# Seed stores and the second unit's queries on GpSimd's DMA queue, and earlier loads of the first unit's operands

## The chip, the cores and the metric

One Trainium2 chip; the kernel runs on 1 of its 8 cores. The metric is device time in microseconds, lower is better.

## The reference

Two independent blocks, whose results are laid side by side. Block A is an S4D convolution: kernels K are built from complex exponentials and convolved with u by FFT. Block B is attention with 16 heads of 28 dimensions over 2048 positions, without a mask. All data are float32.

```python
# A: L = 2048, D = 448, N = 256
dt = exp(log_dt);  A = -exp(log_A_real) + 1j * A_imag;  C = (C_real + 1j * C_imag) * dt[:, None]
P = exp((A * dt[:, None])[:, :, None] * arange(L))
K = 2 * einsum("dn,dnl->dl", C, P).real
y = irfft(rfft(u_t, 2 * L) * rfft(K, 2 * L))[:, :, :L]      # then y + u * D_skip
# B: S = 2048, D = 448, H = 16
q, k, v = split(x @ wqkv)
p = softmax(q @ k.T * 28 ** -0.5)
b = (p @ v) @ wo
out = concatenate([a, b], axis=-1)
```

## The kernel before

The work has an opening and a main loop.

**The main loop** goes over 16 units. A unit u is one group g of four heads (G = 4 groups) and one chunk c of 512 queries (NQ = 4 chunks), and each unit takes 16 steps over tiles of 128 keys. In a step, TensorE makes the scores of four heads (`s_mm`), ScalarE takes their exponentials, and TensorE multiplies the previous step's exponentials with v (`pv_step`). Alongside run the row maxima of the next unit (`max_mm`), the S4D kernels (`k_start`, `e_power` on GpSimd, `g_powers` on VectorE, `k_mm`), and the FFT stages of block A. Its instructions are kept in program order.

**The opening** has two streams. In it the order is not that of the program: a scheduler orders each engine's queue, SyncE's queue of DMA issues included.

- *Projections.* For each chunk of 512 positions (`c` in 0..3), `transposes` turns x, `qk_proj` makes keys and queries of the four groups as a high and a low part (`hl`, two buffers), and `v_proj` makes v. They are stored to DRAM (`k_d`, `q_d`, `v_d`); chunks 0 and 1 also give the key differences `kd_d` (tile `dhl`). Forty-eight such jobs are spread over the first `PW` = 37 of 41 slots.
- *Seeds.* In eight groups (`seeds(o)`, four slots apart) the first powers of the complex exponentials are made. GpSimd makes the sizes `tri` (mg), the first products (`e_base`, `g_base`) and the last complex products (`e5`, tiles `qhat` and `x_e`); ScalarE the sines and exponentials; VectorE the phases and the rest. A group's results lie in two tiles: `se`, a buffer of the pool of query tiles (name `qhat`, three buffers, shared with the queries proper), and `sg` (two buffers). `put_e` and `put_g` store them to `sd_d`, from where the main loop reloads them as `sdb`.

At the end of the opening the operands of the first unit are loaded: `load_kd` (key differences, tiles `kdif0` to `kdif3`), `load_q` (queries, tile `qhat`), `load_k` (keys, tile `khat`, four tiles of four loads each; two tiles from ScalarE's queue, two from SyncE's). `ahead[A0 + i]` and `ahead[A1 + i]` say in which slots the key differences and the first queries are issued. Then come the maxima of unit 0: 16 query tiles of 128 rows, four matmuls each (`max_mm`), of which three are reduced on VectorE. The negated maxima are written into two rows of the queries (`max_put`), and the main loop begins.

In the profile every recorded operation has line 75, that of a helper; operations are told apart by their tiles. SyncE's queue is "SPq", GpSimd is "POOL".

Of the kernel before, what the change touches and what calls it, by code (L numbers as in the profile page):

```python
# [8 lines left out]
F32 = mybir.dt.float32  # L9
F32R = mybir.dt.float32r  # L10
# [13 lines left out]
HG = H // G  # L24
CQ = 512
NQ = L // CQ
# [14 lines left out]
PS = 1  # L41
SGB, XB, XL = 2, 5, 4
K0, KP, KD, UP = 0, 3.5, 5, 3
A0, A1 = 26, 34

N1 = 32
N2 = 64
# [9 lines left out]
F_G = 256  # L57
# [33 lines left out]
def body(ctx, tc, a, out):  # L91
    nc = Engines(tc)
# [4 lines left out]
    def pool(stack, name, bufs=1, space=None, side=None):  # L97
        kw = {} if space is None else {"space": space}
        if side:
            kw["side"] = side  # L100
        return stack.enter_context(tc.tile_pool(name=name, bufs=bufs, reuse_waits="tile", **kw))
# [3 lines left out]
    kd_d = [dram.tile([2, 128, CQ], F32, name=f"kd_{g}") for g in range(G)]  # L105
    q_d = [[dram.tile([2, 128, CQ], F32, name=f"q_{g}_{c}") for c in range(NQ)] for g in range(G)]
    sd_d = [dram.tile([BO, 128, SDF], F32, name=f"sd_{o}") for o in range(NO)]
# [24 lines left out]
    kd_p = pool(att, "kd_p", side="right")  # L132
# [8 lines left out]
    kt_g, kd_g, q_u, m_u, mh_u, o_u, rl_u = {}, {}, {}, {}, {}, {}, {}  # L141

    def load_k(g, j, p, queue=nc.sync):
        t = p.tile([128, L], F32R, name="khat", bufs=HG)
        for r in range(4):
            queue.dma_start(t[32 * r:32 * r + 32, :].bitcast(F32), k_d[g][r % 2, 32 * j:32 * j + 32, :])
        kt_g.setdefault(g, []).append(t)
# [3 lines left out]
    def load_v(g, c):  # L151
        v_g[g, c] = t = v_p.tile([128, NK // NQ, HG, 32], F32, name="v", bufs=5)
        nc.sync.dma_start(t.rearrange("p t h e -> p t (h e)"), v_d[c][:, g])

    def load_kd(g, j, rows=range(4)):
        if 0 in rows:
            kd_g[g, j] = kd_p.tile([128, CQ], F32R, name=f"kdif{j}")
        t = kd_g[g, j]
        for r in rows:
            nc.sync.dma_start(t[32 * r:32 * r + 32].bitcast(F32), kd_d[g][r % 2, 32 * j:32 * j + 32, :])  # L160

    def load_q(u, rows=range(4)):
        g, c = divmod(u, NQ)
        if 0 in rows:
            q_u[u] = q_p.tile([128, HG, CQ], F32R, name="qhat", bufs=3)
        t = q_u[u]
        for r in rows:
            nc.sync.dma_start(t[32 * r:32 * r + 32].bitcast(F32), q_d[g][c][r // 2].rearrange("(j p) q -> p j q", j=HG))

    def max_mm(u, i, kc, ps=w_tile):  # L170

# [37 lines left out]
    with ExitStack() as st:  # L209
# [50 lines left out]
        t = a["A_log_dt"]  # L260
# [51 lines left out]
        def seeds(o):  # L312

            q = {}
# [92 lines left out]
            def cmul(e, dst, s0, n, wr, wi, conj):  # L407

                if e is nc.vector:
                    x_ = ps_x.tile([128, CQ], F32, name="px")[:, :BO * 16 * n].rearrange("p (b h e) -> p b h e", h=16, e=n)  # L410
                else:
                    x_ = s_p.tile([128, BO, 16, 4], F32, name="x_e")[:, :, :, :n]
                br, bi = (w_[:, :, :, None].to_broadcast([128, BO, 16, n]) for w_ in (wr, wi))
                for c in range(2):
                    mul(e, dst[c], s0[c], br)
                    mul(e, x_, s0[1 - c], bi)
                    e.tensor_tensor(dst[c], dst[c], x_, ALU.add if (c == 0) == conj else ALU.subtract)
# [2 lines left out]
            e8 = lambda *i: sl(q["e8"], *i)  # L420
            e3 = lambda: cmul(vec if o % 8 < E3 else pol, e8(3, 4), e8(1, 2), 1, q["e8"][:, :, 0, :, 2], q["e8"][:, :, 1, :, 2], False)
            e5 = lambda: cmul(pol, e8(5, 8), e8(1, 4), 3, q["e8"][:, :, 0, :, 4], q["e8"][:, :, 1, :, 4], False)
            put_e = lambda: nc.sync.dma_start(sd_d[o][:, :, :F_G].rearrange("b p f -> p b f"), q["se"])
            put_g = lambda: nc.sync.dma_start(sd_d[o][:, :, F_G:].rearrange("b p f -> p b f"), q["sg"])

            def load():
                if o not in nats:
# [68 lines left out]
        for c in range(NQ):  # L496
# [4 lines left out]
            if c + 1 < NQ:  # L501
                jobs[1] = (lambda c, f: lambda: (load_x(c + 1), f())[1])(c, jobs[1])
            work += jobs
        stages = [seeds(o) for o in range(NO)]
        n_stage = SP * (NO - 1) + len(stages[0])
        slots = [[] for _ in range(n_stage)]
# [4 lines left out]
        pend, n_work = [], len(work)  # L511

        ahead = collections.defaultdict(list)
        for i in range(2 * HG):
            ahead[A0 + i].append(lambda i=i: load_kd(0, i // 2, range(2 * (i % 2), 2 * (i % 2) + 2)))
        for i in range(2):
            ahead[A1 + i].append(lambda i=i: load_q(0, range(2 * i, 2 * i + 2)))

        def project():

            e = work.pop(0)() if work else None
            while pend:
                pend.pop(0)()
            if e:
                pend.append(e)

        for t in range(n_stage):
            while work and n_work - len(work) < n_work * (t + 1) / PW:
                project()
            for f in slots[t] + ahead.get(t, []):  # L530
                f()
            if t + 1 == PW:
                project()
                wst.close()
                k0_p = pool(k0_st, "k0_p", side="right")
                for j in range(HG):
                    load_k(0, j, k0_p, nc.scalar if j < 2 else nc.sync)
                load_q(1)
                for c in range(NQ):
                    load_v(0, c)  # L540
        xst.close()
        more = [lambda: ps_t.tile([128, CQ], F32, name="pt")] * 2 + [w_tile] * 3
        for i in range(16):
# [444 lines left out]
    for s in range(NS):  # L988
        u, kt = divmod(s, NK)
# [15 lines left out]
        if sm < NS and sm // NK % NQ == NQ - 1 and sm % NK % 4 == 0 and sm % NK and sm // (NQ * NK) + 1 < G:  # L1005
            load_kd(sm // (NQ * NK) + 1, sm % NK // 4 - 1)
        if sm < NS and sm % (NQ * NK) == 0 and sm:
            load_kd(sm // (NQ * NK), HG - 1)
        if kt % 4 == 1 and u % NQ == 1 and u // NQ + 1 < G:
            load_k(u // NQ + 1, kt // 4, k_pools[(u // NQ + 1) % 2])  # L1010
        if kt == 2:
            if u + 2 < NU:
                load_q(u + 2)
# [97 lines left out]
```

## Time and profile before

| | us |
|---|---|
| median of 3 runs | 1360.99 (1358.85 to 1361.72) |
| profiled execution | 1363.72 |
| its span in the trace | 1361.9 |

| engine | busy us, share of the span |
|---|---|
| PE (TensorE matmul) | 1243.9, 91% |
| DVE (VectorE) | 991.3, 73% |
| ACT (ScalarE) | 966.1, 71% |
| POOL (GpSimd) | 839.5, 62% |

Busy shares are means over stages with different limits, so the views that follow are taken by stretches of time. All DMAs of compute data are issued from SyncE's queue, but for eight key loads from ScalarE's. A row of a timeline gives start and duration in us, engine, operation, output tile and input tile, a count, and in brackets the idle time of that engine before it and what ended it. A row of a queue (SPq, ACTq) is the issue of a DMA, not its transfer.

### The profile page before, as it was taken

The page shows a single profiled execution, that of the slowest core. Times are in us where ns is not written, and L with a number is a line of the kernel's source. Part 1 is how long each engine was busy: PE and PEld are TensorE (multiplying, and loading weights), DVE is VectorE, ACT ScalarE, POOL GpSimd, SP SyncE. Part 2 cuts the span into 40 slices and gives each one's busy share as a digit, 9 for nine tenths or more (in the row PEclk, how much of TensorE's full clock was granted, in tenths as well). Part 3 has the DMA queues.
Part 4 walks back from the last instruction along what each step waited for, and adds up shares of the span by engine and source line. Part 5 has one row for each costly group of instructions (what it writes and reads, how often), then busy time and mean ns, then how long its engine had stood idle before and what let it go on. Part 6 is the DMA issues. An engine that isn't in the chain of part 4 may idle for free.

```text
span 1361.9 us, 33142 instructions
## 1 busy us (share of the span) xinstructions
PE 1243.9 (91%) x12625; PEld 709.8 (52%) x12625; DVE 991.3 (73%) x2138; ACT 966.1 (71%) x2067; POOL 839.5 (62%) x705
## 2 busy tenths in 40 slices
PE   6878885799999999999999999999998999998997
PEld 5657762455555555555555555555555545544433
DVE  5897886877777777777788888888887766857311
ACT  4876752488888888888888887878786655655553
POOL 3685681278877878878888988888895111202221
PEclk9988987899999999999999999999999999999999
DMA  6677669636675545378534233632325534636476
GB/s 197 199 261 266 225 212 271 179 74 150 147 164 118 128 135 159 111 202 198 162 94 97 56 73 86 146 79 67 79 65 140 189 116 161 206 111 203 138 192 176
DMA packets 200089, 205.36 MB, mean 151 GB/s; under 512 B 95993, under 2 KB 158521, under 8 KB 197881
## 3 DMA queue, kind: packets, MB, share of 16 engines
q1 hardware_dynamic: 199544, 201.13, 53.2%
q10 hardware_dynamic: 384, 2.10, 0.6%
q8 instruction: 100, 1.64, 0.5%
q14 instruction: 61, 0.49, 0.1%
HBM read 120.73 MB, written 82.18 MB: 149 GB/s over the span
## 4 chain that ended last, share of the span: by engine, by line
PE 61%; DVE 17%; ACT 12%; issue 3%; DMA 3%; POOL 3%; SPq 0%; ACTq 0%; DVEq 0%; POOLq 0%
PE pm L75 35%; PE po L75 13%; PE pss L75 12%; ACT p L75 6%; DVE mx L75 4%; DVE g L75 2%; DVE tri L75 2%; ACT rl L75 2%; DVE p L75 2%; POOL qhat L75 1%; DVE pr L75 1%; DVE zg L75 1%; DVE rl L75 1%; DVE sg L75 1%; ACT tri L75 1%
## 5 line engine op out<-in xcount | busy, mean ns | idle before, releaser
L75 ACT ACTIVATE p<-pss 128x512 f32<-128x512 f32 x1024 | 565.4, 609 | 138.5 <-PE pss L75 127.5
L75 PE MATMUL pss<-qhat,khat 128*128 128x512 f32 x1024 | 403.1, 400 | 3.3 <-ACT p L75 3.3
L75 DVE TENSOR_REDUCE mx<-pm 128x1 f32<-128x512 f32 x500 | 321.4, 683 | 116.3 <-PE pm L75 115.1
L75 PE MATMUL pm<-khat,qhat 128*128 128x512 f32 x749 | 330.1, 444 | 41.4 <-DVE mx L75 36.5
L75 POOL TENSOR_TENSOR e<-e,sdb 128x256 f32<-128x256 f32 x168 | 201.8, 1201 | 171.9 <-ACT e L75 162.9
L75 PE MATMUL po<-p,v 128*32 128x512 f32 x2048 | 271.9, 599 | 0.0
L75 POOL TENSOR_TENSOR e<-e,eu 128x256 f32<-128x256 f32 x168 | 248.1, 1477 | 13.2
L75 PEld LDWEIGHTS pm<-khat,qhat 128*128 128x128 f32 x749 | 142.0, 190 | 216.0 <-DVE mx L75 79.8
L75 PEld LDWEIGHTS pss<-qhat,khat 128*128 128x128 f32 x1024 | 191.1, 189 | 46.7 <-ACT p L75 11.2
L75 DVE CUSTOM_DVE_ANT_0 rl<-pm,rl 128x512 f32<-128x512 f32 x249 | 171.4, 688 | 48.3 <-ACT rl L75 43.8
L75 POOL TENSOR_TENSOR eu<-e,sdb 128x256 f32<-128x256 f32 x168 | 201.7, 1201 | 0.0
L75 DVE TENSOR_TENSOR g<-g,zg 128x128 f32<-128x128 f32 x392 | 162.9, 416 | 46.3 <-ACT zg L75 41.3
L75 ACT ACTIVATE rl<-pm 128x512 f32<-128x512 f32 x249 | 151.2, 607 | 20.7 <-PE pm L75 18.8
L75 POOL TENSOR_TENSOR p<-pr,pr 64x448 f32<-64x448 f32 x32 | 40.9, 1277 | 191.6 <-DVE pr L75 180.5
L75 PE MATMUL pm<-kdif,qhat 128*128 128x512 f32 x249 | 101.6, 408 | 2.2 <-DVE mx L75 1.5
L75 PEld LDWEIGHTS pm<-e,g 128*32 128x32 f32 x3584 | 63.0, 110 | 52.8 <-issue 30.8
L75 DVE TENSOR_TENSOR zg<-g,zg 128x128 f32<-128x128 f32 x224 | 87.5, 391 | 1.9
L75 PEld LDWEIGHTS po<-p,v 128*32 128x32 f32 x2048 | 56.6, 110 | 42.7 <-issue 38.0
L75 PE MATMUL pm<-xh,wh 112*128 112x512 f32 x128 | 56.8, 448 | 22.3 <-DVE hl L75 10.8
L75 PE MATMUL pm<-e,g 128*32 128x64 f32 x3584 | 72.5, 220 | 0.0
L75 ACT ACTIVATE y<-pm 128x448 f32<-128x448 f32 x48 | 26.3, 548 | 63.0 <-PE pm L75 30.7
L75 DVE TENSOR_TENSOR pr<-pm,ub 128x448 f32<-128x448 f32 x64 | 37.0, 619 | 32.7 <-PE pm L75 32.7
(137 smaller groups left out, 1571.8 us busy)
## 6 DMA issues: line engine op xcount, KB each, us to landing
sdb<-sd SPq DMA_DIRECT2D x56, 336.0 KB
qhat<-q SPq DMA_DIRECT2D x64, 256.0 KB
khat<-k SPq DMA_DIRECT2D x56, 256.0 KB
sd<-sg SPq DMA_DIRECT2D x8, 1456.0 KB
k<-hl SPq DMA_DIRECT2D x16, 512.0 KB
q<-hl SPq DMA_DIRECT2D x16, 512.0 KB
mw<-in_mw SPq DMA_DIRECT2D x16, 512.0 KB
sd<-qhat SPq DMA_DIRECT2D x8, 896.0 KB
```

Source lines behind the costliest of these rows:

```text
L75: i = f(*args, **kw)
```

## The change

- `put_e` and `put_g` issue the seed stores from GpSimd's queue instead of SyncE's (16 stores). So do the four loads of the second unit's queries, `load_q(1)`.
- The key differences of all four heads lie in one tile. Those of the first group are loaded by four loads, each for all heads, instead of sixteen; those of the later groups as before, head by head, into slices of that tile.
- The first key differences are issued from slot 27 on (before: from slot 26 in eight pieces), the first queries from slot 25 (before: 34).
- `load_q(1)` and the four `load_v(0, c)` stand behind the loop over the slots, ahead of the maxima, instead of inside it behind the key loads.

As the scheduler orders the opening's queues, the change moves more than its lines. In the new order the loads of v stand on SyncE's queue directly behind the stores of the chunk they read, the first one ahead of the second chunk's stores. All first-unit query loads stand ahead of the last chunk's key stores. On GpSimd the stores stand between the products, and the memsets of a group's seeds stand shortly behind the store whose buffer they reuse. In the main loop the order changes only at its first steps: the row maxima's store into the queries (`qhat<-mh`) stands behind two seed reloads, eight loads of u and one query row of unit 2.

```diff
-A0, A1 = 26, 34
+A0, A1 = 27, 25
...
-    def load_kd(g, j, rows=range(4)):
-        if 0 in rows:
-            kd_g[g, j] = kd_p.tile([128, CQ], F32R, name=f"kdif{j}")
-        t = kd_g[g, j]
-        for r in rows:
-            nc.sync.dma_start(t[32 * r:32 * r + 32].bitcast(F32), kd_d[g][r % 2, 32 * j:32 * j + 32, :])
-
-    def load_q(u, rows=range(4)):
+    kd_t = kd_p.tile([128, HG, CQ], F32R, name="kdif")
+
+    def load_kd(g, j):
+        kd_g[g, j] = kd_t[:, j, :]
+        for r in range(4):
+            nc.sync.dma_start(kd_t[32 * r:32 * r + 32, j, :].bitcast(F32), kd_d[g][r % 2, 32 * j:32 * j + 32, :])
+
+    def load_kd_row(r, g=0, t=kd_t):
+
+        kd_g.update({(g, j): t[:, j, :] for j in range(HG)})
+        nc.sync.dma_start(t[32 * r:32 * r + 32].bitcast(F32), kd_d[g][r % 2].rearrange("(j p) q -> p j q", j=HG))
+
+    def load_q(u, rows=range(4), queue=nc.sync):
...
-            nc.sync.dma_start(t[32 * r:32 * r + 32].bitcast(F32), q_d[g][c][r // 2].rearrange("(j p) q -> p j q", j=HG))
+            queue.dma_start(t[32 * r:32 * r + 32].bitcast(F32), q_d[g][c][r // 2].rearrange("(j p) q -> p j q", j=HG))
...
-            put_e = lambda: nc.sync.dma_start(sd_d[o][:, :, :F_G].rearrange("b p f -> p b f"), q["se"])
-            put_g = lambda: nc.sync.dma_start(sd_d[o][:, :, F_G:].rearrange("b p f -> p b f"), q["sg"])
+            put_e = lambda: nc.gpsimd.dma_start(sd_d[o][:, :, :F_G].rearrange("b p f -> p b f"), q["se"])
+            put_g = lambda: nc.gpsimd.dma_start(sd_d[o][:, :, F_G:].rearrange("b p f -> p b f"), q["sg"])
...
-        for i in range(2 * HG):
-            ahead[A0 + i].append(lambda i=i: load_kd(0, i // 2, range(2 * (i % 2), 2 * (i % 2) + 2)))
+        for i in range(4):
+            ahead[A0 + i].append(lambda i=i: load_kd_row(i))
         for i in range(2):
             ahead[A1 + i].append(lambda i=i: load_q(0, range(2 * i, 2 * i + 2)))
...
                 for j in range(HG):
                     load_k(0, j, k0_p, nc.scalar if j < 2 else nc.sync)
-                load_q(1)
-                for c in range(NQ):
-                    load_v(0, c)
+        load_q(1, queue=nc.gpsimd)
+        for c in range(NQ):
+            load_v(0, c)
         xst.close()
```

## The prediction

> **What bounds the kernel now.** I read the page first, then the windows of the opening stretch, then the queues in it.
>
> ```profile
> span 1361.9 us, 33142 instructions
> ...
> PE 61%; DVE 17%; ACT 12%; issue 3%; DMA 3%; POOL 3%; SPq 0%; ACTq 0%; DVEq 0%; POOLq 0%
> ...
> 60.75:198.00 137.25, 113.37 (x490) 90.69 (x489) 114.78 (x191) 95.03 (x194) 97.72 (x107) 0.90 0.71 239
> ...
> 200.00:210.00 10.00, 4.31 (x16) 3.10 (x15) 7.31 (x17) 1.28 (x2) 6.83 (x8) 0.84 1.02 332
> ...
> 209.00:218.00 9.00, 0.15 (x1) 0.18 (x2) 0.00 (x0) 0.95 (x4) 0.00 (x0) 0.50 1.04 243
> ...
> 218.00:252.00 34.00, 26.86 (x68) 13.23 (x68) 30.04 (x67) 9.78 (x17) 0.00 (x0) 0.89 0.93 259
> ```
>
> The columns of a window are its length, busy time of PE, weight loads, DVE, ACT and POOL, granted clock, DMA share, GB/s. Over the whole span the matrix engine carries the chain. The change touches only what comes before the main loop, about 258 us of 1361.9. That part has three pieces: projections and seeds to 208 us, where PE and DVE are each busy for over 80% of the time and no engine alone bounds; a hole from 209 to 218 where every engine stands and the DMA share is 1.04; then the 48 maxima of the first unit on DVE (30.04 of 34 us). The hole is where this change can earn something.
>
> ```profile
> 203.91 0.40 PE L75 MATMUL pm<-xl,wh 112*128 112x512 f32 x1
> ...
> 217.85 0.77 PE L75 MATMUL pt<-kdif,qhat 128*128 128x512 f32 x1 [13.54 <-DMA qhat<-q]
> ...
> 207.73 0.69 DVE L75 TENSOR_TENSOR hl<-pm,hl 128x512 fp32r<-128x512 f32 x1 [0.44 <-ACT hl L75]
> ...
> 219.50 1.29 DVE L75 TENSOR_REDUCE mx<-pm 128x1 f32<-128x512 f32 x2 [11.09 <-PE pm L75]
> ...
> 199.84 0.47 SPq L75 DMA_DIRECT2D qhat<-q  x1
> 200.74 0.49 SPq L75 DMA_DIRECT2D q<-hl  x1
> 201.28 0.51 SPq L75 DMA_DIRECT2D sd<-sg  x1
> 210.57 0.80 SPq L75 DMA_DIRECT2D qhat<-q  x2
> 211.46 0.38 SPq L75 DMA_DIRECT2D k<-hl  x1
> 211.94 0.42 SPq L75 DMA_DIRECT2D sd<-qhat  x1
> ...
> 215.45 2.60 SPq L75 DMA_DIRECT2D khat<-k  x2
> ...
> 204.11 1.60 ACTq L75 DMA_DIRECT2D khat<-k  x2
> ...
> 207.12 9.75 ACTq L75 DMA_DIRECT2D khat<-k  x5
> ```
>
> The last projection product ends at 204.3 and DVE is done with what precedes the maxima at 208.4. The first matmul of the maxima waits 13.54 us for the queries. Their last two rows stood on SP's queue behind the seventh group's seed store: SP issued it at 201.28 and could issue nothing until 210.57. The first key loads on ACT's queue, the other thing the maxima need, took from 204.11 until 216.87 to be issued.
>
> **Part by part: the tail.** The new order has all four query rows and all four key-difference rows of the first unit on SP's queue a chunk earlier, before the last keys are projected. No seed store remains on SP, so the key and query stores and the key loads follow each other directly. What is late next is the first key tile: four loads that ACT starts at 204.11.
>
> ```profile
> sd<-sg SPq DMA_DIRECT2D x8, 1456.0 KB
> ...
> sd<-qhat SPq DMA_DIRECT2D x8, 896.0 KB
> ...
> khat<-k ACTq DMA_DIRECT2D x8, 256.0 KB
> ...
> qhat<-q SPq DMA_DIRECT2D x64, 256.0 KB
> ```
>
> Those four loads are 1.05 MB. The two windows above move 332 and 243 GB/s; I take 289. The seventh group's seeds (896 and 1456 KB) still travel at that moment, from another queue. If the two queues share evenly, the loads take 2.1 MB / 289 GB/s = 7.3 us and are there at 211.4, 6.4 us before 217.85. If nothing shared, they would take 3.6 us and the end of DVE's earlier work, 208.4, would be the limit: 9.5 us. I take 6.4. Each further key tile has to come within a quarter of the 34 us window, 8.5 us; at the halved rate it needs 7.3, so the maxima keep their pace and the gain passes on to the main loop.
>
> ```profile
> 251.67 1.26 SPq L75 DMA_DIRECT2D qhat<-mh  x2
> ...
> L75 PE MATMUL pss<-qhat,khat x5: 398/449/632, 258.3 to 261.7; 128*128 128x512 f32 x5
> ```
>
> The maxima's rows are put into the queries at 251.67, and the first score product starts at 258.3. In the new order that store stands behind the seed reloads, the eight loads of u and one query row of the third unit, which waits for the last seed store. It is harmless as long as POOL's last store lands before about 245.
>
> **SP's waits before that.** Without seed stores, SP waits less for POOL and DVE, and stores of keys leave earlier.
>
> ```profile
> ACT hl L75 <- DMA k<-hl: 3.0, 1, 3.0
> ...
> 171.85 7.83 SPq L75 DMA_DIRECT2D v<-vst  x2
> ...
> 180.92 0.39 SPq L75 DMA_DIRECT2D k<-hl  x1
> ...
> 186.19 0.67 ACT L75 ACTIVATE hl<-pm,kones 128x512 fp32r<-128x512 f32 x1
> ...
> 60.75 4.12 DMA sd<-qhat
> ```
>
> In 60 to 209 us ACT waited 3.0 us for a key store to release a buffer. I credit half, 1.5 us, between nothing and all. Against it: the v loads no longer come behind the key loads; the scheduler puts them as soon as their stores are issued, and each one makes SP wait until the last v store has landed. For the last v chunk, the store issued at 179.7 is followed by such a load, with the key store of 180.92 behind it. With a landing time of 4.1 us, as the seed store's 4.12, that key store goes at 183.8 and lands at 187.9. Its buffer is wanted at 186.19, so 1.7 us at most; I take 1.4, since the v store is smaller. Below nothing it cannot go, as a wait is only added. The four joined key-difference loads replace sixteen small ones off the path: nothing.
>
> **POOL's queue.** This is the price. Sixteen stores and four query loads now stand between POOL's products, in order. Each of POOL's stalls is passed on: DVE waits for POOL's products, PE for DVE's evictions.
>
> ```profile
> L75 SPq DMA_DIRECT2D sd<-qhat x8: 360/513/1276, 60.7 to 237.7; - x8
> ...
> L75 POOL TENSOR_TENSOR qhat<-qhat x15: 1014/1161/3600, 55.3 to 203.7; 128x336 f32<-128x336 f32 x15
> ...
> 61.54 0.67 POOL L75 TENSOR_TENSOR gz<-tri 128x224 f32<-128x224 f32 x1 [0.82 <-DVE px L75]
> 62.17 1.46 POOL L75 TENSOR_TENSOR qhat<-tri 128x112 f32<-128x112 f32 x3
> ...
> 64.98 0.56 POOL L75 MEMSET qhat<- 128x112 f32 x2 [1.35 <-DMA sd<-qhat]
> ...
> 81.96 2.25 POOL L75 TENSOR_TENSOR tri<-tr,pw 128x1232 f32<-128x1232 f32 x1 [1.98 <-ACT tr L75]
> ```
>
> No POOL issue of a DMA is in this trace. Below it is bounded by SP's issue of the same store, 0.51 us; above by that store's landing time, 4.12 us, since writing 896 rows' worth of descriptors could at worst fill all of it. I take the geometric middle, 1.4 us, and keep both ends.
>
> Then there are waits for landing. A group's seeds reuse the buffer of an earlier group, and its memset stands on POOL shortly behind the store that has to land. In the trace this cost 1.35 us once, because products of 0.67 and 1.46 us stood between. In the new order: right behind the first group's store (4.1 us); behind the second's with a 2.25 us product and a short one between (1.1); behind the fourth's, fifth's and sixth's with about 2.1 us of products between (2.0 each). Together 11.1 us.
>
> Thirteen stores fall between 60.75 and 198, where POOL begins the products of the last group on which DVE and PE still depend. POOL is busy 97.72 of 137.25 us there, so 39.5 us are free. With issue time c the new work is 13c + 11.1, and POOL comes late by 13c - 28.4 us where that is positive. It is free up to c = 2.2. At 1.4 it needs 29.3 of 39.5 us: nothing on the path. The cover is POOL's waiting for ACT's tables and sines; if it is gone, each further 0.1 us of c costs 1.3 us.
>
> **The sum.** -6.4 (tail) - 1.5 (key stores) + 1.4 (v loads) + 0 (POOL) = -6.5 us. The profiled execution took 1363.72 us beside its span of 1361.9, so 1357.2 by it; that execution lies 2.7 us above the median of the three runs, 1360.99, so the forecast is 1354.5 us.
>
> **Rivals.**
> - POOL becomes the bound of the opening. It decides from c = 2.7 us, where 13c - 28.4 eats the 6.5. At c = 4.1 POOL is 24.9 us late and the time is 1360.99 - 6.5 + 24.9 = 1379.4. For it: 896 separate rows in a store, with every free microsecond of POOL needed; against it: 39.5 us free. 0.33.
> - DVE and POOL hinder each other. POOL's 128x336 product takes 1.01 us at best but 3.60 at worst, when DVE is at work beside it. If that doubled the 1.4 us to 2.8, POOL would be 8.0 us late: 1362.5. The Trainium skill (SBUF — State Buffer, the "DVE blocks DMA" trap) says that a DMA from GpSimd's queue is held while DVE runs in a two-port mode, because its descriptors cannot be written, and advises the other queues. The trace bears out the hindrance for products, and cannot show it for descriptors. 0.10, half of it within 0.2%, half slower.
> - The tail is bound by transfers and the key loads come no sooner, as the DMA share stands at 1.04 in the hole: the sum keeps only -1.5 + 1.4, 1360.9. The Trainium skill (DMA: Bandwidth & Descriptors, Issuing engines are not separate DMA queues) states that all issuing engines feed the same 16 DMA engines, so that spreading only saves issue time. Against it: three of the query rows above (199.84 and 210.57, 0.77 MB) leave the tail, and in the hole it was SP's order that held the queries. 0.07, of it 0.04 within 0.2% and 0.03 faster.
>
> **How the numbers follow.** The forecast's case has 0.50. Its own range is 1348.5 (9.5 and 3.0 gained, nothing lost) to 1358. About 0.2% is what a measurement of this kernel can tell, 2.7 us. Faster: 0.50 + 0.03 = 0.53. Same: 0.05 + 0.04 = 0.09. Slower: 0.33 + 0.05 = 0.38. The range reaches from just below the best case, 1347, to c = 4.3, 1382; what is left out is mostly a POOL issue that costs still more.
>
> **What would show it.** Right: the first matmul of the maxima near 211 with a wait for khat instead of qhat, the first score product near 252, POOL's DMA rows near 1.4 us, POOL's waits on DMA near 11 us in total, DVE hardly waiting for POOL. Wrong: POOL over 90% busy between 60 and 200 with its DMA rows above 2.7 us, and the last projection later than 204; or the key loads landing at 217 again; or a main loop, from the first score product to the end, that differs from today's 1103.6 us (1361.9 - 258.3) by more than 2.

## The result, and the profile after

| | before | after |
|---|---|---|
| median (range), on the same chips | 1363.22 (1358.85 to 1366.49) | 1369.15 (1367.02 to 1373.47) |
| runs | 8 | 8 |
| span of the profiled execution | 1361.9 | 1371.7 |

The changed kernel is slower: ratio 1.0051, 95% interval 1.0034 to 1.0067, about 6.9 us. The forecast was 1354.5 us, in a range that holds the result; its sign was wrong.

The windows of the opening after the change, cut where its stages now end (columns as before: length; busy time of PE, weight loads, DVE, ACT, POOL; granted clock; DMA share; GB/s):

```profile
span 1371.7 us, 33150 instructions
...
60.75:198.00 137.25, 112.40 (x470) 89.59 (x468) 105.64 (x174) 88.87 (x177) 94.64 (x111) 0.86 0.72 247
198.00:210.00 12.00, 9.27 (x34) 7.42 (x35) 10.29 (x19) 8.82 (x17) 10.46 (x11) 0.86 0.46 163
210.00:220.00 10.00, 1.88 (x6) 0.84 (x4) 6.32 (x15) 2.24 (x6) 7.36 (x11) 0.71 1.01 337
220.00:252.00 32.00, 21.95 (x52) 11.63 (x52) 23.56 (x51) 7.84 (x16) 5.60 (x7) 0.72 0.91 292
```

In these 137.25 us DVE did 105.64 us of work; before, it did 114.78 in the same stretch. Some 9 us of work are missing and follow behind 198, where DVE and POOL are still busy for most of the window up to 210. TensorE's hole with the DMA share above 1 is still there, from about 211 on instead of 209; VectorE and GpSimd now work in it (6.32 and 7.36 of the 10 us from 210), mostly on the last seeds.

The timeline of the matrix engine after the change: the last projection product, a first product of the maxima on key differences, the first matmul of the maxima on keys, the first score product of the main loop.

```profile
210.69 0.40 PE L75 MATMUL pm<-xl,wh 112*128 112x512 f32 x1
216.17 0.80 PE L75 MATMUL pm<-kdif,qhat 128*128 128x512 f32 x1 [5.09 <-DVE hl L75]
224.44 0.76 PE L75 MATMUL pt<-khat,qhat 128*128 128x512 f32 x1 [7.47 <-DMA khat<-k]
...
266.88 0.63 PE L75 MATMUL pss<-qhat,khat 128*128 128x512 f32 x1
```

Against 203.91 for the last projection, 218.41 for the first key matmul and 258.3 for the main loop before: the projections end 6.8 us later, the first key matmul follows 13.75 us behind them (before 14.5), and the main loop starts 8.5 us later. The wait between is no longer for queries: TensorE stands 5.09 us for VectorE's key and query parts (`hl`), then 7.47 us for keys. The maxima themselves, from the first key matmul to their store, take 35.6 us, before 33.3. From the main loop's start to the end of the span it is 1104.8 us, before 1103.6.

The timeline of POOL after the change, around the first and the fourth group's stores, then DVE's:

```profile
60.35 1.09 POOL L75 DMA_DIRECT2D sd<-qhat  x1 [0.31 <-POOL qhat L75]
66.83 0.33 POOL L75 MEMSET qhat<- 128x112 f32 x1 [5.39 <-DMA sd<-qhat]
67.00 0.66 POOL L75 TENSOR_TENSOR gz<-tri 128x224 f32<-128x224 f32 x1
67.62 1.19 POOL L75 TENSOR_TENSOR qhat<-tri 128x112 f32<-128x112 f32 x3
...
137.51 0.97 POOL L75 DMA_DIRECT2D sd<-qhat  x1 [0.30 <-DVE hl L75]
...
145.40 0.30 POOL L75 MEMSET qhat<- 128x112 f32 x1 [5.07 <-DMA sd<-qhat]
```

```profile
68.46 0.57 DVE L75 TENSOR_TENSOR px<-qhat 128x112 f32<-128x112 f32 x1 [5.56 <-POOL qhat L75]
...
148.36 3.21 DVE L75 TENSOR_TENSOR qhat<-qhat 128x112 f32<-128x112 f32 x2 [2.62 <-POOL qhat L75]
```

POOL issues the store of a seed tile and stands until it has landed, because the next instruction on its queue writes into the same buffer: the memset of a group whose turn comes later (with three buffers, the first pair waited for is that of the fourth group). Behind the memset stand the products that the current group needs, and DVE waits for those: 5.39 us of POOL's wait come out as 5.56 us of DVE's. The waits from 60 to 262 us, first before, then after (total, times, longest, in us):

```profile
DVE qhat L75 <- POOL qhat L75: 2.9, 3, 2.3
DVE sg L75 <- POOL tri L75: 2.2, 4, 0.6
POOL qhat L75 <- DMA sd<-qhat: 1.4, 1, 1.4
DVE px L75 <- POOL qhat L75: 1.0, 2, 0.7
```

```profile
POOL qhat L75 <- DMA sd<-qhat: 15.6, 6, 5.4
ACT hl L75 <- DMA k<-hl: 9.7, 4, 3.7
DVE px L75 <- POOL qhat L75: 8.4, 3, 5.6
...
DVE sg L75 <- POOL tri L75: 6.7, 3, 4.9
DVE qhat L75 <- POOL qhat L75: 6.6, 5, 3.4
```

DVE's waits for POOL rose from 6.1 to 21.7 us in these rows.

### The profile page after: what moved, and what is told of

Its sections match the earlier page's. It is cut to its first block, busy times and chain, and to the rows that moved or that the text cites. A ratio compares the mean times of both kernels' runs of the same rounds, so it can differ in the third digit from the quotient of the medians.

```text
span 1371.7 us, 33150 instructions
## 1 busy us (share of the span) xinstructions
PE 1250.5 (91%) x12625; PEld 714.0 (52%) x12625; DVE 992.4 (72%) x2138; ACT 968.7 (71%) x2069; POOL 851.8 (62%) x725
## 3 DMA queue, kind: packets, MB, share of 16 engines
q8 instruction: 100, 1.64, 0.5%
## 4 chain that ended last, share of the span: by engine, by line
PE 59%; DVE 15%; ACT 12%; DMA 5%; issue 4%; POOL 4%; SPq 1%; ACTq 0%; POOLq 0%; DVEq 0%
PE pm L75 34%; PE po L75 13%; PE pss L75 12%; ACT p L75 6%; DVE mx L75 4%; DVE g L75 2%; ACT rl L75 2%; DMA k<-hl 2%; DVE p L75 2%; POOL qhat L75 2%; DVE pr L75 1%; DVE tri L75 1%; DVE qhat L75 1%; DVE zg L75 1%; DMA khat<-k 1%
## 5 line engine op out<-in xcount | busy, mean ns | idle before, releaser
L75 PEld LDWEIGHTS pss<-qhat,khat 128*128 128x128 f32 x1024 | 191.4, 189 | 45.4 <-issue 11.1
```

The costliest lines, as they stand in the source:

```text
L75: i = f(*args, **kw)
```

## The experiments

Ratios are to the kernel before on the same chips, with 95% intervals. The last three columns are starts in the profiled execution, in us. `nc.kept` names queues whose instructions stay in the program's order from there on; elsewhere the scheduler orders the opening. A column is one execution: before and e8, equal in time, differ by 0.9 to 1.6 us in the last three, so smaller differences there say nothing.

| run | what | median us | ratio | last projection | first key matmul | store of the maxima |
|---|---|---|---|---|---|---|
| before | | 1363.22 | 1 | 203.91 | 218.41 | 251.67 |
| after | | 1369.15 | 1.0051 | 210.69 | 224.44 | 260.02 |
| e1 | v loads behind the keys | 1366.1 | 1.0026 | 208.13 | 221.70 | 254.26 |
| e2 | memsets in their group's place | 1360.65 | 0.9985 | 202.03 | 216.94 | 249.40 |
| e3 | both | 1361.04 | 0.9979 | 203.56 | 216.91 | 249.49 |
| e5 | e3, tail cleared | 1357.39 | 0.9952 | 203.82 | 213.22 | 245.67 |
| e6 | before, with stores on GpSimd | 1366.7 | 1.0028 | 207.98 | 220.22 | 252.66 |
| e8 | before, with e2's edit | 1361.81 | 0.9998 | 202.30 | 216.97 | 250.80 |
| e9 | e3, queries late | 1370.08 | 1.0046 | 205.47 | 219.03 | 256.98 |

### Where the 6.9 us went: memsets and v loads

```diff
 # e1
+        nc.kept = ("sync",)
         for c in range(NQ):
             load_v(0, c)
+        nc.kept = KEPT["p"]
 # e2, in places()
+                nc.kept = ("gpsimd",)
                 pol.memset(q["e8"][:, :, 0, :, 0], 1.0)
                 pol.memset(q["e8"][:, :, 1, :, 0], 0.0)
+                nc.kept = KEPT["p"]
 # e3: both
```

> The changed kernel with the four loads of v held on SyncE's queue behind the first unit's key loads, as they stood before the change. Theory V (the v loads, moved between the projection stores, make SyncE wait for the v stores to land and so hold back the last chunk's key and query stores): the last chunk's first key store goes near 183 us instead of 189.9, the last projection ends near 206 instead of 211, time 4 to 6 us below the changed kernel, about the kernel before. Theory M (GpSimd stands still at memsets that wait for a store just issued, 15.6 us in six waits): the projections still end near 211, time within 1.5 us of the changed kernel.

> The changed kernel with the memsets of the seed buffers held in program order on GpSimd, so that each waits for a store one group earlier. Theory M: GpSimd's waits for stores fall from 15.6 us to under 4, the last projection ends near 205 and the time falls by 5 to 7 us to that of the kernel before. Theory V: those waits go, but the projections still end at 209 to 211, time within 2 us of the changed kernel.

> Both of these together. If V and M are all that the change lost in the opening: projections end at 204 or a little sooner. Then theory K (the key loads themselves, 4 MB beside seed stores and queries, set the start of the maxima: 13.3 us after the last projection in both kernels) expects the time of the kernel before, within 3 us. My prediction's theory (the queries behind a seed store set it) expects 6 us less than the kernel before.

Measured: e1 1.0026 (1.0013 to 1.0039), e2 0.9985 (0.9968 to 1.0002), e3 0.9979 (0.9965 to 0.9994). POOL's timeline and the waits of e2:

```profile
39.79 0.56 POOL L75 MEMSET qhat<- 128x112 f32 x2
59.80 1.09 POOL L75 DMA_DIRECT2D sd<-qhat  x1 [0.31 <-POOL qhat L75]
60.88 0.58 POOL L75 MEMSET qhat<- 128x112 f32 x2
61.30 0.68 POOL L75 TENSOR_TENSOR gz<-tri 128x224 f32<-128x224 f32 x1
```

```profile
DVE px L75 <- POOL qhat L75: 5.3, 5, 2.5
...
POOL qhat L75 <- DMA sd<-qhat: 3.3, 1, 3.3
DVE sg L75 <- POOL tri L75: 2.3, 3, 1.3
```

The same memset right behind the same store (59.80, 60.88) waits for nothing, since it now belongs to the next group and writes a buffer that is long free. POOL's waits for stores fall from 15.6 to 3.3 us, the projections end at 202.03, and the ratio falls by 0.0066, 9 us. DVE's waits for POOL in the rows above fall from 21.7 to 8.5 us. That is more than the whole loss, and the two intervals lie apart: the memsets' place is its main cause. Holding the v loads back gives 3.4 us while the memsets are out of place (e1; its interval still overlaps that of the changed kernel) and nothing once they are in place (e2 against e3), although the v loads of e2 stand just as early. Nor did e1 go as the theory of the v loads had it: with no v load ahead, the last chunk's first key store left at 188.31, not near 183. With e2's edit on the kernel before, nothing moves:

> The kernel before with nothing but the memsets in order: a control for the pin. GpSimd waited there for a store once, 1.4 us. Theory M expects no change, within 2 us; if this is 4 us or more faster, the pin helps by itself and the comparison of the pinned changed kernel with the kernel before is not fair.

Measured: e8, the kernel before with e2's edit, 1361.81 us, 0.9998 (0.998 to 1.0016). The gain is not the pin's own.

### The tail: are the keys late because of bytes, of queues, or of ScalarE's issuing?

In e3 everything ahead of the tail is as good as before, and the queries are there; still the first key matmul comes 13.35 us behind the last projection. ACT's queue and PE in e3:

```profile
203.75 0.35 ACTq L75 DMA_DIRECT2D khat<-k  x1
...
206.71 8.57 ACTq L75 DMA_DIRECT2D khat<-k  x7
```

```profile
203.56 0.39 PE L75 MATMUL pm<-xl,wh 112*128 112x512 f32 x1
...
216.91 0.77 PE L75 MATMUL pt<-khat,qhat 128*128 128x512 f32 x1 [8.05 <-DMA khat<-k]
```

```diff
 # e5 = e3 and:
+        held = []
+        hold = lambda f, late_: (lambda: held.append(f)) if late_ else f
...
-                    ... [put_g], [put_e]]
+                    ... [hold(put_g, o >= 6)], [hold(put_e, o == 7)]]
...
-        load_q(1, queue=nc.gpsimd)
+        load_q(1)                      # on SyncE, in order: behind the keys
         for c in range(NQ):
             load_v(0, c)
+        for f in held:
+            f(nc.sync)
 # e10 = e5 with load_q(1, queue=nc.gpsimd) as in the change
 # e11 = e5 with nc.scalar if j < 1 else nc.sync in load_k's call (was j < 2)
 # e12 = the changed kernel with that edit
```

> The changed kernel with both pins (v behind the keys, memsets in order), and the rest of the tail cleared for the key loads: the second unit's queries, the seventh group's larger store and both stores of the eighth group go on SyncE's queue behind the key loads and v. About 1.9 MB leave the 13 us between the last projection and the first key matmul. Theory K, by transfers (the key loads share the DMA engines with that data): the first key matmul comes 4 to 6 us sooner, near 211, and the time falls 3 to 5 us below the one with both pins. Theory K, by issue or latency (the loads are held by ScalarE's queue and by each load's own landing, not by bytes) or by VectorE's last seed products, which end at 215: no more than 1.5 us.

Measured: 1357.39 us, 0.9952 (0.9937 to 0.9968), the lowest ratio here, 3.7 us ahead of e3, with intervals that just touch. ACT's queue and PE:

```profile
204.06 0.34 ACTq L75 DMA_DIRECT2D khat<-k  x1
...
207.48 4.78 ACTq L75 DMA_DIRECT2D khat<-k  x7
```

```profile
203.82 0.63 PE L75 MATMUL pm<-xl,wh 112*128 112x512 f32 x1
...
212.50 0.79 PE L75 MATMUL pm<-kdif,qhat 128*128 128x512 f32 x1 [7.81 <-DVE hl L75]
213.22 0.77 PE L75 MATMUL pt<-khat,qhat 128*128 128x512 f32 x1
```

The seven key loads are out in 4.78 us instead of 8.57, the key matmul comes 9.4 us behind the last projection and waits for no load: what is late next is DVE (`hl`, 7.81 us). In e3 the DMA engines moved 4.1 MB in those 13.35 us (306 GB/s), in e5 2.4 MB in 9.4 us. By e3's issues, at most 2.5 MB of what was moved out had stood there: the second unit's queries (1.05 MB) and the seventh group's larger store (1.49 MB). Which of the transfers mattered most is not separated: SyncE's eight key loads, too, left later in e5, from 212.94 on instead of 208.51. But the key loads of ScalarE's queue were held up by transfers that other queues had issued. That is what the Trainium skill states (DMA: Bandwidth & Descriptors, Issuing engines are not separate DMA queues): all issuing engines feed the same 16 DMA engines and their DMAs interleave; the traces agree, with 13.35 against 9.4 us.

> The kernel of e5 with the second unit's queries issued from GpSimd's queue again; the three seed stores stay behind v on SyncE. If the tail goes by bytes, whatever the queue: 1.05 MB come back of the 3.4 MB that e5 took out, at 289 GB/s 3.6 us of transfers, of which e5 left some unused (its key matmul waited for VectorE, not for the keys): the first key matmul at 214 to 216 us instead of 213.2 and a ratio of 0.9955 to 0.9975. If only the stores' 2.4 MB mattered: 213.2 and 0.995. If the queries alone mattered: 216.9 and 0.998, as e3.

Measured: 1358.13 us, 0.9963 (0.995 to 0.9976), in the range of the first case; but the first key matmul was at 212.81, near that of the second. The last projection came at 200.80 in this execution, so the wait is 12.0 us, between e5's 9.4 and e3's 13.35, but hardly for keys: TensorE stood 9.18 us for VectorE (`hl`) and 0.98 us for a key load, and of the four query loads two (204.66, 207.01) had been issued well before, the third only at 212.07. So e10 does not tell bytes from stores, and its time does not separate it from e5.

> The changed kernel with the second key tile issued from SyncE's queue instead of ScalarE's, so that ScalarE issues four key loads instead of eight. In the changed kernel ScalarE was held by the issue of seven of them from 213.84 to 229.7, while the maxima that it evicts began at 224.4, and these took 35.6 us instead of the 32.5 of e3 (first key matmul to the store of the maxima). If ScalarE's own issuing is what stretches the maxima: ScalarE free by about 219, maxima 32.5 us, 3 us gained, ratio 1.002 to 1.004. If the transfers are the limit and the issue only shows their backlog: the second tile is as late from the other queue, the maxima stay at 35 us or more and the ratio at 1.005 or above.

> The kernel of e5 with the same edit. There ScalarE was free at 212.3, before the maxima began, so its issuing costs nothing: by the first theory no gain, ratio 0.994 to 0.996. SyncE can issue the second tile only behind the last key and query stores (212.9), some 3 us later than ScalarE did: if that tile is then late for the fifth group of maxima, 1 to 3 us lost, ratio 0.996 to 0.998.

These two asked whether ScalarE's own issuing stretches the maxima. The changed kernel's ACT queue, and that of e12:

```profile
213.84 15.87 ACTq L75 DMA_DIRECT2D khat<-k  x7
229.75 0.37 ACT L75 ACTIVATE sg<-pn 128x112 f32<-128x112 f32 x1 [15.34 <-DVE mx L75]
```

```profile
212.99 5.17 ACTq L75 DMA_DIRECT2D khat<-k  x3
218.21 0.37 ACT L75 ACTIVATE sg<-pn 128x112 f32<-128x112 f32 x1 [4.64 <-DVE sg L75]
```

Measured: e12 1372.99 us, 1.0084 (1.0059 to 1.011); e11 1356.99 us, 0.9962 (0.9946 to 0.9977). In e12 ScalarE was free at 218.2, as asked, and the maxima still took 36.1 us (224.16 to 260.28; the changed kernel 35.6, e3 32.6). So freeing ScalarE is not enough. But e12 does not refute the theory either, since it puts another wait in place of the first: the last of the moved loads now stand behind SyncE's last key and query stores, and in the middle of the maxima TensorE waits for a key load:

```profile
233.09 0.47 PE L75 MATMUL pm<-khat,qhat 128*128 128x512 f32 x1 [3.27 <-DMA khat<-k]
```

In the changed kernel that wait is 1.64 us. Over all traces, the maxima took 35.6 to 38.0 us in the four (changed, e4, e7, e9) in which ScalarE was still issuing key loads when the first key matmul began, and 32.4 to 33.8 us in the others, e12 apart. That goes with both readings, as late keys and a long issue come together. In e11 the key matmul waited 1.66 us for keys again and nothing was won.

### What the early queries are worth

```diff
 # e6 = before, with the stores on GpSimd and the memsets in order (e2), and
+                nc.kept = ("sync",)
                 load_q(1)
                 for c in range(NQ):
                     load_v(0, c)
+                nc.kept = KEPT["p"]
 # e9 = e3 with A0, A1 = 27, 34 instead of 27, 25
```

> The kernel before with one part of the change alone, and without its two stalls: seed stores on GpSimd's queue, memsets in order, the second unit's queries and v held behind the key loads on SyncE's queue. First key differences and first queries stay where they were before the change. If the early queries and joined differences bring nothing (theory K), the time is that of the changed kernel with both pins, within 2 us. If they bring what I forecast, this is about 6 us slower than that one, as its first matmul waits for queries.

> The kernel of e3 with one number changed: the first unit's queries are issued from slot 34 again instead of 25. Early queries help ahead of the projections' end (the reading of e6): the query loads stand among the last key stores on SyncE again, the last projection product starts near 207.5 us instead of 203.6, and the ratio is 1.001 to 1.003. Rival: e6 lost its time by the sixteen small key-difference loads and by the second unit's queries on SyncE, not by the queries' slot: the last projection stays near 203.6 and the ratio at 0.998. Second rival: with four queries late in the tail the first key matmul comes later too, at over 13 us behind the last projection, and the ratio is above 1.004.

Measured: e6 1366.7 us, 1.0028 (1.0011 to 1.0044); e9 1370.08 us, 1.0046 (1.0029 to 1.0063), above the interval of the first theory and inside the second rival's, though not by the rival's mechanism: the key matmul came 13.56 us behind the last projection, e3's 13.35. One number, the slot of the first queries, is worth 0.67% in e3's frame, 9 us. By e9's and e3's anchors, 1.9 us of the 7.5 us at the store of the maxima lie ahead of the projections' end, 0.2 in the wait, 5.4 in the maxima (37.95 us instead of 32.58); only the last is well beyond what single executions differ by. ACT's timeline in e9, then PE's, shows where these 5.4 went:

```profile
209.80 16.60 ACTq L75 DMA_DIRECT2D khat<-k  x6
226.45 0.36 ACT L75 ACTIVATE sg<-pn 128x112 f32<-128x112 f32 x1 [16.07 <-DMA khat<-k]
```

```profile
227.88 1.59 PE L75 MATMUL pt<-khat,qhat 128*128 128x512 f32 x2 [4.49 <-ACT rl L75]
```

ScalarE issues key loads until 226.40 and can evict none of the maxima before; TensorE stands 4.49 us for that. Here ScalarE's issuing is on the path, whatever made it long. This is no fixed price of late queries: e6, with queries as late, had ScalarE free at 219.1, ahead of its first key matmul, and its maxima took 32.4 us.

### The stores back on SyncE

```diff
 # e4 = the changed kernel with put_e and put_g on nc.sync; e7 = e4 with e2's edit
```

> The changed kernel with the seed stores back on SyncE's queue; the second unit's queries stay on GpSimd's, the first key differences and queries stay early. Here the scheduler puts the v loads late again by itself, and GpSimd waits for no store of its own. V and M both expect the changed kernel's loss gone: the time of the kernel before or a little less. K expects no more than 2 us of gain from the early queries; my prediction's theory about 6 us of gain. If the loss stays, it is neither V nor M.

> The run with the stores on SyncE's queue and everything else of the change, 18 us slower than the kernel before, with the memsets in order. GpSimd waited 15.8 us there in three waits, 11.6 at once, since the early queries take one of the three buffers that the seeds use. If the place of the memsets was the cause (theory M), the loss falls to under 5 us. If it is the lost buffer with stores that SyncE issues late (theory B), most of it stays, 10 us or more.

Measured: e4 1381.76 us, 1.0130 (1.0107 to 1.0154), which no theory had; e7 1379.07 us, 1.0120 (1.0098 to 1.0142). POOL's row behind e4's late store, then e7's:

```profile
207.37 0.56 POOL L75 MEMSET qhat<- 128x112 f32 x2 [11.59 <-DMA sd<-qhat]
```

```profile
203.88 0.55 POOL L75 MEMSET qhat<- 128x112 f32 x2 [10.75 <-DMA sd<-qhat]
```

The memsets' place is not the cause here. The reading that fits: the early queries take one of the three seed buffers for the rest of the opening, so a seed store has to leave at once; SyncE's queue, with other transfers waiting ahead of it, lets it go late (in e4 a seed tile that GpSimd had finished at 173.75 was stored at 197.00), and the last group's memset stands for 11 us wherever it is put. So the parts of the change depend on each other: stores on GpSimd with late queries cost 0.3% (e6) and 0.5% (e9), the rest of the change without them 1.2% (e7), and all together, with the memsets and v in place, is 0.2% faster than before (e3).

## Why the prediction was wrong, by its steps

- **POOL at nothing: the step that failed.** The sum of POOL's new work was about right: 12 issues of 0.97 us and 13.5 of the 15.6 us of landing waits lie ahead of 198, together 25.1 us, where 13 issues of 1.4 us and 11.1 us had made 29.3 (the waits listed there add to 11.2; nothing hangs on it). The criterion was wrong. I set that sum against all of POOL's free time, 39.5 us, and called the rest hidden. But idle time covers a wait only where it lies: in POOL's waits for ACT's tables, between groups. The landing waits stood elsewhere, directly ahead of products that DVE was waiting for. My own sentence, that each of POOL's stalls is passed on, was not followed. The price: 6.8 us at the projections' end, gone in e2.
- **POOL as the bound (rival 1).** The outcome, a late POOL, came, but not the mechanism: it was to decide from an issue time of 2.7 us, and at 0.97 us its formula gives no lateness at all. That the range holds the result is owed to the price of this rival, and is luck. **DVE hindering GpSimd's DMAs (rival 2)** is not seen: the 20 issues of the opening took 0.58 to 1.09 us, with DVE busy for 77% of the stretch. The Trainium skill (SBUF — State Buffer, the "DVE blocks DMA" trap) has such issues held up while DVE is in a two-port mode; no row here shows a held issue, and whether DVE was in such a mode beside one can't be read from them.
- **The tail at -6.4.** The first half was right: no wait for queries is left. The second, keys at 211.4, failed: they came 13 us after the last projection, as in the transfer rival (0.07), and the argument against that rival, that three query rows leave the tail, was too weak. I reckoned 2.1 MB between the start of the key loads and their arrival; the 13.35 us of e3 moved 4.1 MB, since the second unit's queries, the seventh group's seeds, SyncE's key loads and the last keys and queries travel then too. It also missed that ACT's second key load stands behind the evictions of the last keys and queries (203.75, then 206.71 in e3). e5 shows that 3.7 us were there, for a change that takes transfers out of the tail.
- **Key stores at -1.5.** Against it: ACT's waits for key stores rose from 3.0 to 9.7 us, and to between 9.5 and 14.0 us in e2, e3, e5 and e6 (6.3 in e1). Some of these stores take longer to land: the last chunk's first left at 180.92 before and at 180.74 in e3, but its buffer was free by 186.19 before and only at 188.78 in e3. Why is not settled; that the seed stores now travel beside them is only argued.
- **v loads at +1.4.** 3.4 us in e1, nothing once the memsets are in place. The first key store of the last chunk, forecast at 183.8, left at 189.89; in e2, with the v loads as early, at 180.28, and in e1, with the v loads late, at 188.31. So it was POOL's lateness, not the v loads, that held most of it.
- **Joined key differences at nothing, first steps of the main loop at nothing.** The main loop was 1.2 us longer, within the 2 us given. The key differences were not tried by themselves.
- **Early queries.** Counted in the tail only. They are worth some 9 us in e3's frame (e9), mostly in the maxima, which the prediction had keep their pace: there ScalarE, still issuing key loads, made TensorE wait. In the changed kernel the maxima took 2.3 us longer than before; in e2 (32.5 us) they did not.

Of the 6.9 us, then, shown are +9 from the memsets' place. The remaining -2 (e2, whose interval reaches no change) are the balance of stores on GpSimd, which cost, and queries early, which gain; the split of that balance is known only for whole kernels. Why moved stores cost 4 to 6 us where the queries are late (e6, e9) stays open.

## What to carry to other kernels

A wait is weighed against the slack at the place where it stands, not against the engine's idle time in the whole stage: look at who waits for the instruction right behind it. When a store goes to the queue of the engine that also refills its buffer, look where the scheduler puts the refill; an instruction without inputs, such as a memset, is pulled ahead until only the store holds it. And when one late load at the end of a stage is cured, count every transfer in flight at that moment against the next one, whichever queue issued it, and look which engine is held while it issues the late loads.

## What the runs showed of the hardware

An issue from GpSimd's queue cost 0.97 us for a seed store and 0.58 to 0.61 for a query load; 896 and 1456 KB cost the same. These stores landed late beside other traffic: the page's rows of the changed kernel (KB each, us to landing in the median) are:

```profile
sd<-sg POOLq DMA_DIRECT2D x8, 1456.0 KB, 8.9
...
sd<-qhat POOLq DMA_DIRECT2D x8, 896.0 KB, 4.8
```

Over all 16 seed stores the trace gives 4.8, 6.8 and 14.9 us for the shortest, middle and longest. The one landing time that I had from before, 4.12 us, lay below them all.
